# A Strassen-type first stage whose input sums get a buffer for the third sum and start at the first plain product, and whose weight differences are handed out in steps

## The chip, the cores and the metric

One core of one Trainium2 chip runs the whole program. The metric is the device time of one execution in microseconds (us). Engines are named as in the profile: PE (TensorE, matrix products; PEld is its weight load), DVE (VectorE), ACT (ScalarE), POOL (GpSimd) and SP (SyncE, which here only issues transfers). The kernel before takes 853.27 us, the median of 3 runs (851.54 to 855.01).

## The reference

Inputs are float32 and the products are wanted to float32 accuracy. What matters here is the middle of three parts:

```python
attn = softmax(q @ k^T / 8 + bias)          # B=2, H=8, S=576, D=64
x = (attn @ v) as [N=1152 tokens, 512]
for e in range(4):                          # first stage, w1[e]: 512x1024, w2[e]: 1024x512
    h = max(x @ w1[e], 0)
    out += p[:, e:e+1] * (h @ w2[e])
h = out @ w_in                              # second stage, w_in: 512x2048, w_out: 2048x512
g = (a0 + a1*h + a2*h^2 + a3*h^3) / (1 + |b0||h| + |b1|h^2 + 1e-6)
return g @ w_out
```

`p` are the normalised shares of the four experts.

## The kernel before, in words

Accuracy comes from splitting: a float32 matrix is held as a high part in the PE's reduced float32 format and a low part (value minus high), and a product is three products, high*high, high*low and low*high. A split costs one ACT copy (high) and one subtraction on DVE or POOL (low).

The program has three phases. The bias and attention come first, ordered by a planner with costs and due times (`Flow`). At its end `x` lies in SBUF, transposed, as four blocks `x[b, c]`: b is the batch half (576 tokens) and c the half of the 512 input channels, each with a high and a low part of [128, 2, 576] (k = 0, 1 are the two 128-channel slices). Then comes `first_stage`, whose order is written out by hand, and then `second_stage`.

`first_stage` goes through 16 pairs p of hidden blocks: pair p is 256 of the 4096 hidden columns, two blocks f of 128. A pair's "up" part makes h for both f and both b; its "down" part `down(p, t)` (L853) is six 512-column products for token tile t = 0..8, after which DVE adds `prob * ps` to `acc` (L865 for p = 0, L867 after that). Pairs 0 and 1 are "plain": `plain(p, f, b)` (L896) is 24 products of 288 columns into PSUM bank x or y by turns. Pairs 2 to 15 use a Strassen-type scheme, `seven(p)` (L971): seven block products of 12 matmuls instead of eight, on blocks of x and on sums of blocks:

- s1 = x10 + x11, s2 = s1 - x00, s4 = x01 - s2 and s3 = x00 - x10 (each split into high and low);
- the order of the seven products by what they read is x00, x01, s2, s1, s3, s4, x11; they accumulate in the two banks x and y, so that a bank is begun again only after DVE and ACT have taken what was in it. `keep` (L964, ACT) copies a bank into the temporaries m1, u2 or m5, `finish` (L968, DVE) adds one of these to a bank, and `relu` (L891 ACT, and later L892 DVE through `late` and `flush`) writes h in two parts. The next pair's first product starts bank y anew, so it waits for L892 of the last product.

Between two of the seven products stands one `down` of the pair before; after the seventh stand two more (t = 7 and 8).

Three kinds of side work are put between these by hand, each on the in-order queues of DVE, ACT and POOL:

- `sum_steps` (L928) makes the sums in 36 steps, one instruction each: `whole` (L917, high plus low, DVE), `combine` (L920, DVE), `high` (L923, ACT) and `low` (L926, on DVE for k = 0, on POOL for k = 1). `tick(n)` (L1004) issues the next n steps. The third sum s3 is written over x[1, 0], so its steps stand last, after the last plain product has been issued.
- `conv_f64` (L305) turns the second stage's float64 weights into float32, five steps for a piece: ACT L313, DVE L315, L317, L319, L321, and then a store from SP. It uses `tick` too once the sums are done.
- `load_w` (L250) splits the weights of a later pair: ACT L273 and POOL L277 for the down weights, and `load_differences` (L281) for the up weights of pairs 2 and later, which the scheme needs as seven blocks, four of them differences: four POOL subtractions (L290), three ACT copies (L293, on 256, 512 and 1024 elements), three POOL subtractions for the low parts (L295, same sizes), and then `stage_w`, which has SP fetch a later chunk of weights into the staging buffer that came free. Within a pair `load_w` stands after the second product (down weights) and after the fourth (the next pair's up weights, all of it at once).

Of the kernel before, what the change touches and what calls it, by code (L numbers as in the profile page):

```python
# [18 lines left out]
B, H, S, D, HID = 2, 8, 576, 64, 32  # L19
# [4 lines left out]
NPAIR = E * FF // 256  # L24
P = 128
# [99 lines left out]
class Kernel:  # L125
# [124 lines left out]
    def load_w(self, n=1, defer=lambda fn: fn()):  # L250


        for _ in range(n):
            if self.w_next < len(self.w_plan):
                i = self.w_next
                self.w_next += 1
                key, _, a, b = self.w_plan[i]
                stg = self.w_staged.pop(0)
                if key[0] == "u" and len(key) == 2 and key[1] > 1:
                    self.load_differences(key, stg)  # L260
                else:
                    self.load_parts(i, key, a, b, stg, defer)

    def load_parts(self, i, key, a, b, stg, defer):
        nc = self.nc
# [12 lines left out]
            self.stage_w()  # L278
        defer(low)

    def load_differences(self, key, stg):  # L281


        nc = self.nc
        wu = self.w_tiles[key] = self.up.tile([P, 2, 7, 2, P], F32R, tag="wu", bufs=2, name="wu")
        wt = self.up.tile([P, 4, 2, P], F32, tag="wt", bufs=1, name="wt")
        blocks = stg.rearrange("p (x k) (n f) -> p x n k f", x=2, n=2)
        (a, b), (c, d) = ([blocks[:, x, n] for n in range(2)] for x in range(2))
        for out, x, y in ((0, b, a), (2, d, b), (1, d, wt[:, 0]), (3, c, wt[:, 1])):
            nc.gpsimd.tensor_tensor(out=wt[:, out], in0=x, in1=y, op=ALU.subtract)  # L290
        parts = ((slice(0, 1), blocks[:, 0, 0:1]), (slice(1, 3), blocks[:, 1]), (slice(3, 7), wt))
        for sl, x in parts:
            nc.scalar.activation(out=wu[:, 0, sl], in_=x, func=AF.Copy)  # L293
        for sl, x in parts:
            nc.gpsimd.tensor_tensor(out=wu[:, 1, sl], in0=x, in1=wu[:, 0, sl].bitcast(F32), op=ALU.subtract)  # L295
        self.stage_w()

    def stage_f64(self):
# [570 lines left out]
    def first_stage(self):  # L869
# [3 lines left out]
        nc = self.nc  # L873
# [3 lines left out]
        def flush():  # L877
            while late:
                late.pop(0)()
# [16 lines left out]
        def plain(p, f, b):  # L896
            if b == 0:
                self.h_pair(p, f)
            ps = bank("xy"[plain_no[0] % 2])
            plain_no[0] += 1  # L900
            for half in range(2):
                for k in range(4):
                    self.up_part(ps[:, half, 0:288], p, f, b, half, k)
            flush()
            relu(p, f, b, ps[:, :, 0:288], True)

        sums = self.up.tile([P, 3, 2, 2, S], F32R, tag="s", bufs=1, name="sums")
        s1, s2, s4 = ((sums[:, i, 0], sums[:, i, 1]) for i in range(3))  # L910
        s3 = self.x[1, 0]

        def temp(tag):
            return self.up.tile([P, S], F32, tag=tag, bufs=1, name=tag)

        def whole(t, x, k):
            nc.vector.tensor_tensor(out=t, in0=x[0][:, k].bitcast(F32), in1=x[1][:, k].bitcast(F32), op=ALU.add)  # L917

        def combine(t, x, y, op):
            nc.vector.tensor_tensor(out=t, in0=x, in1=y, op=op)  # L920

        def high(t, s, k):
            nc.scalar.activation(out=s[0][:, k], in_=t, func=AF.Copy)  # L923

        def low(t, s, k):
            (nc.vector, nc.gpsimd)[k].tensor_tensor(out=s[1][:, k], in0=t, in1=s[0][:, k].bitcast(F32), op=ALU.subtract)  # L926

        def sum_steps():  # L928
            x = self.x
            for k in range(2):  # L930
                t, v, w = temp("m1"), temp("u2"), temp("m5")
                yield whole(t, x[1, 0], k)
                yield whole(v, x[1, 1], k)
                yield combine(t, t, v, ALU.add)
                yield high(t, s1, k)
                yield whole(v, x[0, 0], k)
                yield low(t, s1, k)
                yield combine(v, t, v, ALU.subtract)
                yield high(v, s2, k)
                yield whole(w, x[0, 1], k)  # L940
                yield low(v, s2, k)
                yield combine(w, w, v, ALU.subtract)
                yield high(w, s4, k)
                yield low(w, s4, k)
            for k in range(2):
                t, v = temp("m5"), temp("u3")
                yield whole(t, x[0, 0], k)
                yield whole(v, x[1, 0], k)
                yield combine(t, t, v, ALU.subtract)
                yield high(t, s3, k)  # L950
                yield low(t, s3, k)

        def product(ps, p, x, i, start, stop):
            wu = self.w_tiles["u", p]
            for k in range(2):
                for j, (w, v) in enumerate(((0, 0), (0, 1), (1, 0))):
                    for half in range(2):
                        nc.tensor.matmul(ps[:, half, 0:288], lhsT=wu[:, w, i, k], rhs=x[v][:, k, 288 * half:288 * half + 288],  # L958
                                         start=(start and k == j == 0), stop=(stop and k == 1 and j == 2), skip_group_check=True)
            flush()  # L960

        def keep(ps, tag):
            m = temp(tag)
            nc.scalar.activation(out=two(m), in_=ps[:, :, 0:288], func=AF.Copy)  # L964
            return m
# [5 lines left out]
        def seven(p):  # L971


            x = self.x
            self.h_pair(p, 0)
            self.h_pair(p, 1)
            y = bank("y")
            product(y, p, x[0, 0], 0, True, False)
            m1 = keep(y, "m1")
            yield  # L980
            z = bank("x")
            product(z, p, x[0, 1], 1, True, True)
# [12 lines left out]
            product(z, p, s4, 2, False, True)  # L995
            finish(p, 1, 0, z, u2)
            yield
            product(y, p, x[1, 1], 6, False, True)
            relu(p, 0, 1, y[:, :, 0:288], True)
            yield  # L1000

        side = sum_steps()

        def tick(n=1):  # L1004
            for _ in range(n):
                next(side, None)

        plain(0, 1, 0)
        self.load_w()
        plain(1, 0, 0)  # L1010
        plain(1, 1, 0)
        plain(0, 0, 1)
        tick(2)
        plain(0, 1, 1)
        tick(2)
        flush()
        self.load_w()
        for t in range(9):
            if t in (3, 6):
                plain(1, t // 3 - 1, 1)  # L1020
                tick(2)
            flush()
            self.down(0, t)
            tick(1 if t > 5 else 3)
            if t == 2:
                self.load_w()
        flush()
        self.stage_f64()
        self.stage_f64()
        for p in range(2, NPAIR):  # L1030
            for i, _ in enumerate(seven(p)):
                if p == 2 and i == 2:
                    assert next(side, 0) == 0
                    side = self.conv_f64()
                tick(3 if p == 2 and i < 2 else 1)
                flush()
                self.down(p - 1, i)
                tick(3 if p == 2 and i < 2 else i < 5)
                if i == 1 or i == 3 and p < NPAIR - 1:
                    self.load_w()  # L1040
            if p < NPAIR - 1:
                self.down(p - 1, 7)
                self.down(p - 1, 8)
# [193 lines left out]
```

## Time and profile before

| | us |
|---|---|
| median of 3 runs | 853.27 (851.54 to 855.01) |
| the profiled execution, its own time | 850.36 |
| its span in the trace | 848.5 |
| PE busy in the span | 803.2 (95%) |
| DVE busy | 696.9 (82%) |
| ACT busy | 500.0 (59%) |
| POOL busy | 469.4 (55%) |

The profiled execution took 1.9 us more than its span. Busy times are sums over instructions; the four engines work at the same time. The plain products of pairs 0 and 1 begin at 233.31 us in the span, pair 2 at 270.58 us, and the last of pair 15's seven products at 606.47 us. Idle time is given in the trace with the instruction that ended it.

### The profile page before, as it was taken

The page shows a single profiled execution, that of the slowest core. Times are in us where ns is not written, and L with a number is a line of the kernel's source. Part 1 is how long each engine was busy: PE and PEld are TensorE (multiplying, and loading weights), DVE is VectorE, ACT ScalarE, POOL GpSimd, SP SyncE. Part 2 cuts the span into 40 slices and gives each one's busy share as a digit, 9 for nine tenths or more (in the row PEclk, how much of TensorE's full clock was granted, in tenths as well). Part 3 has the DMA queues.
Part 4 walks back from the last instruction along what each step waited for, and adds up shares of the span by engine and source line. Part 5 has one row for each costly group of instructions (what it writes and reads, how often), then busy time and mean ns, then how long its engine had stood idle before and what let it go on. Part 6 is the DMA issues. An engine that isn't in the chain of part 4 may idle for free.

```text
span 848.5 us, 13528 instructions
## 1 busy us (share of the span) xinstructions
PE 803.2 (95%) x4980; PEld 691.7 (82%) x4980; DVE 696.9 (82%) x1162; ACT 500.0 (59%) x932; POOL 469.4 (55%) x398
## 2 busy tenths in 40 slices
PE   6989999998998899999999999999999899899997
PEld 2438888887897798888889889888888799789996
DVE  7978888888649888878988788889678878888885
ACT  6998898887523333333333333332368787878773
POOL 3287777777237544344555544344158977565552
PEclk9999999999999899999999999999999899999999
DMA  6777757461003143334343433334121211000011
GB/s 170 245 275 203 181 112 182 108 180 51 1 25 100 34 144 112 122 124 124 125 133 124 142 111 100 125 124 124 51 100 50 100 51 51 0 1 1 1 38 74
DMA packets 67522, 87.36 MB, mean 103 GB/s; under 512 B 33409, under 2 KB 41985, under 8 KB 67329
## 3 DMA queue, kind: packets, MB, share of 16 engines
q1 hardware_dynamic: 66880, 86.35, 33.7%
q8 instruction: 39, 0.64, 0.3%
q14 instruction: 27, 0.21, 0.1%
q10 hardware_dynamic: 576, 0.16, 0.1%
HBM read 60.12 MB, written 21.36 MB: 96 GB/s over the span
## 4 chain that ended last, share of the span: by engine, by line
PE 47%; DVE 20%; ACT 16%; issue 10%; POOL 6%; DMA 1%; SPq 0%; POOLq 0%; DVEq 0%; ACTq 0%
PE ps_o L861 11%; PE ps_y L958 6%; PE ps L660 5%; PE ps_o L1110 5%; PE ps_x L958 5%; PE ps_h L1102 5%; PE ps L550 3%; PE ps L610 3%; DVE pp L1091 2%; DVE rr L1090 2%; ACT rr L1087 2%; POOL qq L1085 2%; ACT hid L369 2%; DVE hs L892 2%; ACT bo L398 2%
## 5 line engine op out<-in xcount | busy, mean ns | idle before, releaser
L861 PE MATMUL ps_o<-we,hs 128*128 128x512 f32 x810 | 204.5, 394 | 0.0
L861 PEld LDWEIGHTS ps_o<-we,hs 128*128 128x128 f32 x810 | 146.9, 189 | 26.0
L277 POOL TENSOR_TENSOR we<-wstg,we 128x1024 fp32r<-128x1024 f32 x20 | 49.4, 2468 | 188.7 <-ACT we L273 188.7
L867 DVE SCALAR_TENSOR_TENSOR acc<-ps_o,prob,acc 128x512 f32<-128x512 f32 x135 | 98.2, 743 | 21.8 <-PE ps_o L861 21.6
L1085 POOL TENSOR_TENSOR qq<-qq,ha 128x384 f32<-128x384 f32 x48 | 58.4, 1216 | 66.2 <-ACT qq L1082 66.2
L1110 PE MATMUL ps_o<-wmh,hs 128*128 128x512 f32 x252 | 85.2, 396 | 9.3 <-POOL hs L1094 5.3
L958 PEld LDWEIGHTS ps_y<-x,wu 128*128 128x128 f32 x504 | 70.6, 188 | 9.3 <-DVE hs L892 6.7
L958 PE MATMUL ps_y<-x,wu 128*128 128x288 f32 x504 | 74.4, 296 | 2.8 <-DVE hs L892 2.5
L593 POOL TENSOR_SCALAR P<-P,ri 128x576 f32<-128x576 f32 x72 | 53.3, 752 | 39.4 <-DVE ri L582 26.9
L1102 PE MATMUL ps_h<-x,wmh 128*128 128x384 f32 x288 | 75.0, 341 | 0.0
L1110 PEld LDWEIGHTS ps_o<-wmh,hs 128*128 128x128 f32 x252 | 47.8, 190 | 21.7 <-POOL hs L1094 7.0
L564 DVE CUSTOM_DVE_ANT_0 P<-ps,bias 128x576 f32<-128x576 f32 x72 | 53.4, 749 | 10.8 <-PE ps L550 10.3
L572 ACT ACTIVATE P<-P,nm 128x576 f32<-128x576 f32 x72 | 55.6, 774 | 9.2 <-DVE nm L564 7.2
L1089 DVE SCALAR_TENSOR_TENSOR qq<-qq,rr 128x384 f32<-128x384 f32 x48 | 33.0, 688 | 30.1 <-ACT rr L1088 28.8
L380 PE MATMUL ps_ab<-hid,wm 128*32 128x288 f32 x576 | 47.7, 426 | 9.8 <-DVE hid L372 7.6
L1094 POOL TENSOR_TENSOR hs<-pp,hs 128x384 fp32r<-128x384 f32 x48 | 52.6, 1096 | 7.2 <-issue 6.2
L641 DVE TENSOR_TENSOR ptl<-ps,pth 128x512 fp32r<-128x512 f32 x72 | 51.1, 725 | 6.4 <-ACT pth L637 5.4
L1102 PEld LDWEIGHTS ps_h<-x,wmh 128*128 128x128 f32 x288 | 53.7, 192 | 2.0
L958 PE MATMUL ps_x<-sums,wu 128*128 128x288 f32 x336 | 50.4, 300 | 3.9 <-DVE m L968 3.9
L958 PEld LDWEIGHTS ps_x<-sums,wu 128*128 128x128 f32 x336 | 48.7, 193 | 6.4 <-DVE m L968 4.3
L550 PE MATMUL ps<-kh,qs 128*128 128x288 f32 x168 | 51.6, 327 | 1.2 <-DVE nm L564 0.8
L372 DVE TENSOR_SCALAR hid<-ltab,shift 128x576 f32<-128x576 f32 x108 | 50.2, 541 | 0.0
(145 smaller groups left out, 2054.9 us busy)
## 6 DMA issues: line engine op xcount, KB each, us to landing
wstg<-moe_w SPq DMA_DIRECT2D x32, 512.0 KB, 3.6
bias_d<-bo SPq DMA_DIRECT2D x9, 1152.0 KB, 5.1
bias<-bias_d SPq DMA_DIRECT2D x16, 576.0 KB, 5.0
w<-moe_w_in SPq DMA_DIRECT2D x16, 512.0 KB, 4.0
w<-moe_w_out SPq DMA_DIRECT2D x16, 512.0 KB, 3.7
kl<-kh SPq DMA_DIRECT2D x16, 288.0 KB, 4.8
w_u<-wmag SPq DMA_DIRECT2D x16, 256.0 KB, 2.3
w_d<-wmag SPq DMA_DIRECT2D x16, 256.0 KB, 2.4
```

What stands on the lines that cost most here:

```text
L550: nc.tensor.matmul(ps[:, half, dst:dst + w], lhsT=lhs, rhs=k[:, src:src + w], start=(i == 0), stop=(i == len(m) - 1))
L564: nc.vector.tensor_tensor_reduce(out=Pt[u][:, S * h:S * h + S].rearrange("p (a b) -> p a b", a=2), in0=ps[:, :, 0:288], in1=self.bias_t[n ...
L572: nc.scalar.activation(out=pt, in_=pt, func=AF.Exp, scale=-1.0, bias=stat.pop(g), accum_out=sums[n, c][:, h:h + 1])
L593: nc.gpsimd.tensor_scalar(out=pt[:, sl], in0=pt[:, sl], scalar1=ri, scalar2=1.0, op0=ALU.mult, op1=ALU.mult)
L641: nc.vector.tensor_tensor(out=dl, in0=ps, in1=dh.bitcast(F32), op=ALU.subtract)
L861: nc.tensor.matmul(ps, lhsT=a, rhs=w[:, f, :], start=(f == i == 0), stop=(f == 1 and i == 2))
L867: nc.vector.scalar_tensor_tensor(out=acc[:, t], in0=ps, scalar=pr, in1=acc[:, t], op0=ALU.mult, op1=ALU.add)
L958: nc.tensor.matmul(ps[:, half, 0:288], lhsT=wu[:, w, i, k], rhs=x[v][:, k, 288 * half:288 * half + 288], start=(start and k == j == 0), st ...
L1085: nc.gpsimd.tensor_tensor(out=qq, in0=qq, in1=ha, op=ALU.mult)
L1094: nc.gpsimd.tensor_tensor(out=lo, in0=pp, in1=hi.bitcast(F32), op=ALU.subtract)
L1102: nc.tensor.matmul(ps, lhsT=w[:, k, fo:fo + P], rhs=v[:, k, :], start=(k == i == 0), stop=(k == 3 and i == 2))
L1110: nc.tensor.matmul(ps, lhsT=a[:, P * tt:P * tt + P], rhs=w[:, f % 2, :], start=(f == i == 0), stop=(f == 3 and i == 2))
```

## The change

The buffer `sums` gets a fourth slot, and s3 is written there instead of over x[1, 0]. The steps of the sums are put in another order, 32 in place of 36: the whole blocks x10 and x00 are reused, so four `whole` steps fall away; the low parts of s1 and s2 are made on DVE for both k, those of s3 and s4 on POOL. The steps begin behind the first plain product, three behind each of the first five plain products, two behind each of the others, then two for each of the first six down tiles and one for each of the last three; all are out before pair 2. `conv_f64` therefore has the ticks of pair 2 from its first product on, and from here on its ticks stand on both sides of the down tile for products 0 to 5 and nowhere at product 6 (before: ahead of the down tile for all seven, behind it for the first five).

`load_differences` becomes a generator. In a pair it is opened after the second product, and its pieces are issued after the third (the four POOL subtractions), the fourth (first ACT copy), the fifth (second ACT copy) and the sixth (third ACT copy, all three POOL low parts, and the fetch). For pair 2's own weights it is still run through at once, in `load_w` at t == 2.

```diff
-                    self.load_differences(key, stg)
+                    self.w_next -= 1
+                    for _ in self.load_differences():
+                        pass
...
         for out, x, y in ((0, b, a), (2, d, b), (1, d, wt[:, 0]), (3, c, wt[:, 1])):
             nc.gpsimd.tensor_tensor(out=wt[:, out], in0=x, in1=y, op=ALU.subtract)
-        parts = ((slice(0, 1), blocks[:, 0, 0:1]), (slice(1, 3), blocks[:, 1]), (slice(3, 7), wt))
-        for sl, x in parts:
-            nc.scalar.activation(out=wu[:, 0, sl], in_=x, func=AF.Copy)
-        for sl, x in parts:
-            nc.gpsimd.tensor_tensor(out=wu[:, 1, sl], in0=x, in1=wu[:, 0, sl].bitcast(F32), op=ALU.subtract)
+        yield
+        high(0)
+        yield
+        high(1)
+        yield
+        high(2)
+        for i in range(3):
+            low(i)
         self.stage_w()
...
-        sums = self.up.tile([P, 3, 2, 2, S], F32R, tag="s", bufs=1, name="sums")
-        s1, s2, s4 = ((sums[:, i, 0], sums[:, i, 1]) for i in range(3))
-        s3 = self.x[1, 0]
+        sums = self.up.tile([P, 4, 2, 2, S], F32R, tag="s", bufs=1, name="sums")
+        s1, s2, s3, s4 = ((sums[:, i, 0], sums[:, i, 1]) for i in range(4))
...
             for k in range(2):
-                t, v, w = temp("m1"), temp("u2"), temp("m5")
+                t, v, w, u = (temp(tag) for tag in ("m1", "u2", "m5", "u3"))
                 yield whole(t, x[1, 0], k)
                 yield whole(v, x[1, 1], k)
-                yield combine(t, t, v, ALU.add)
...
+                yield combine(v, t, v, ALU.add)
+                yield high(v, s1, k)
+                yield whole(w, x[0, 0], k)
+                yield combine(t, w, t, ALU.subtract)
+                yield high(t, s3, k)
+                yield low(v, s1, k, nc.vector)
+                yield combine(v, v, w, ALU.subtract)
+                yield high(v, s2, k)
+                yield low(t, s3, k, nc.gpsimd)
+                yield whole(u, x[0, 1], k)
+                yield low(v, s2, k, nc.vector)
+                yield combine(u, u, v, ALU.subtract)
+                yield high(u, s4, k)
+                yield low(u, s4, k, nc.gpsimd)
...
         plain(0, 1, 0)
+        tick(3)
         self.load_w()
-        plain(1, 0, 0)
...
+        for p, f, b in ((1, 0, 0), (1, 1, 0), (0, 0, 1), (0, 1, 1)):
+            plain(p, f, b)
+            tick(3)
         flush()
...
-            tick(1 if t > 5 else 3)
+            tick(1 if t > 5 else 2)
...
+        side = self.conv_f64()
         for p in range(2, NPAIR):
+            weights = iter(())
             for i, _ in enumerate(seven(p)):
-                if p == 2 and i == 2:
-                    assert next(side, 0) == 0
-                    side = self.conv_f64()
-                tick(3 if p == 2 and i < 2 else 1)
+                tick(i < 6)
                 flush()
                 self.down(p - 1, i)
-                tick(3 if p == 2 and i < 2 else i < 5)
-                if i == 1 or i == 3 and p < NPAIR - 1:
+                tick(i < 6)
+                if i == 1:
                     self.load_w()
+                    if p < NPAIR - 1:
+                        weights = self.load_differences()
+                elif i > 1:
+                    next(weights, None)
```

## Rows read from the trace of the kernel before

**Rows 1.** PE's waits from 225 to 610: us in total, times, longest.

```profile
PE ps_x L958 <- DVE m L968: 3.9, 1, 3.9
PE ps_y L958 <- DVE hs L892: 2.5, 5, 0.6
PE ps_o L861 <- DVE acc L865: 2.1, 2, 1.3
```

**Rows 2.** Timeline of PE, pair 2 and start of pair 3: start, duration, line, shapes, [idle before].

```profile
270.58 1.75 PE L958 MATMUL ps_y<-x,wu 128*128 128x288 f32 x12
...
277.43 1.75 PE L958 MATMUL ps_y<-sums,wu 128*128 128x288 f32 x12
...
284.44 3.25 PE L958 MATMUL ps_x<-sums,wu 128*128 128x288 f32 x12 [3.88 <-DVE m L968]
...
290.03 1.75 PE L958 MATMUL ps_y<-x,wu 128*128 128x288 f32 x12
...
293.01 1.75 PE L958 MATMUL ps_x<-sums,wu 128*128 128x288 f32 x12
...
301.66 1.75 PE L958 MATMUL ps_y<-x,wu 128*128 128x288 f32 x12
```

**Rows 3.** Windows: busy us of PE, PEld, DVE, ACT, POOL; granted clock; DMA share, GB/s.

```profile
230.00:240.00 10.00, 10.00 (x64) 9.07 (x63) 1.74 (x3) 2.50 (x5) 2.89 (x3) 0.90 0.00 0
...
264.00:270.58 6.58, 4.53 (x19) 3.07 (x18) 6.55 (x8) 0.83 (x2) 4.37 (x3) 1.00 0.25 80
...
284.44:290.03 5.59, 5.59 (x19) 5.03 (x19) 4.79 (x5) 4.21 (x7) 5.33 (x4) 0.50 0.03 2
663.00:676.00 13.00, 9.21 (x32) 7.71 (x31) 11.36 (x13) 10.60 (x20) 13.00 (x9) 0.74 0.30 96
```

**Rows 4.** Timeline of DVE, sums and first pair.

```profile
244.50 0.75 DVE L917 TENSOR_TENSOR m<-x 128x576 f32<-128x576 f32 x1
...
252.22 2.95 DVE L926 TENSOR_TENSOR sums<-m,sums 128x576 fp32r<-128x576 f32 x1
...
283.63 0.75 DVE L968 TENSOR_TENSOR m<-ps_x,m 128x576 f32<-128x576 f32 x1
```

**Rows 5.** Timelines of PE, ACT and POOL in the plain part.

```profile
246.12 3.34 PE L851 MATMUL ps_x<-x,we 128*128 128x288 f32 x24
...
250.05 0.68 ACT L923 ACTIVATE sums<-m 128x576 fp32r<-128x576 f32 x1
...
261.69 1.04 ACT L293 ACTIVATE wu<-wt 128x1024 fp32r<-128x1024 f32 x1
262.64 0.63 ACT L891 ACTIVATE hs<-ps_y 128x576 fp32r<-128x576 f32 x1
...
251.75 2.80 POOL L277 TENSOR_TENSOR we<-wstg,we 128x1024 fp32r<-128x1024 f32 x1 [10.89 <-ACT we L273]
254.51 2.47 POOL L290 TENSOR_TENSOR wt<-wstg 128x256 f32<-128x256 f32 x2
...
268.37 1.41 POOL L926 TENSOR_TENSOR sums<-m,sums 128x576 fp32r<-128x576 f32 x1 [1.41 <-ACT sums L923]
```

**Rows 6.** Timeline of PE, last down tiles of pairs 2, 3 and 15.

```profile
297.56 4.26 PE L861 MATMUL ps_o<-we,hs 128*128 128x512 f32 x18
...
321.04 4.26 PE L861 MATMUL ps_o<-we,hs 128*128 128x512 f32 x18
...
608.05 4.26 PE L861 MATMUL ps_o<-we,hs 128*128 128x512 f32 x18
```

**Rows 7.** Timelines of POOL, DVE and PE at the end of pair 3.

```profile
318.07 2.91 POOL L295 TENSOR_TENSOR wu<-wt,wu 128x1024 fp32r<-128x1024 f32 x1
...
319.31 1.97 DVE L317 TENSOR_SCALAR wmag<-wmag 128x512 uint32<-128x512 uint32 x1
321.19 0.75 DVE L968 TENSOR_TENSOR u<-ps_x,u 128x576 f32<-128x576 f32 x1
...
324.63 0.75 DVE L892 SCALAR_TENSOR_TENSOR hs<-ps_y,hs 128x576 fp32r<-128x576 f32 x1
```

More of the change, by code (lines that the diff above doesn't have):

```diff
@@ L257, in load_w @@
                 key, _, a, b = self.w_plan[i]
-                stg = self.w_staged.pop(0)
                 if key[0] == "u" and len(key) == 2 and key[1] > 1:
-                    self.load_differences(key, stg)
+                    self.w_next -= 1
+                    for _ in self.load_differences():
+                        pass
                 else:
-                    self.load_parts(i, key, a, b, stg, defer)
+                    self.load_parts(i, key, a, b, self.w_staged.pop(0), defer)
     def load_parts(self, i, key, a, b, stg, defer):
@@ L279, in load_parts, with load_differences @@
         defer(low)
-    def load_differences(self, key, stg):
+    def load_differences(self):
         nc = self.nc
+        key = self.w_plan[self.w_next][0]
+        assert key[0] == "u"
+        self.w_next += 1
+        stg = self.w_staged.pop(0)
         wu = self.w_tiles[key] = self.up.tile([P, 2, 7, 2, P], F32R, tag="wu", bufs=2, name="wu")
@@ L288, in load_differences, with high, low @@
         (a, b), (c, d) = ([blocks[:, x, n] for n in range(2)] for x in range(2))
+        parts = ((slice(0, 1), blocks[:, 0, 0:1]), (slice(1, 3), blocks[:, 1]), (slice(3, 7), wt))
+        def high(i):
+            sl, x = parts[i]
+            nc.scalar.activation(out=wu[:, 0, sl], in_=x, func=AF.Copy)
+        def low(i):
+            sl, x = parts[i]
+            nc.gpsimd.tensor_tensor(out=wu[:, 1, sl], in0=x, in1=wu[:, 0, sl].bitcast(F32), op=ALU.subtract)
         for out, x, y in ((0, b, a), (2, d, b), (1, d, wt[:, 0]), (3, c, wt[:, 1])):
             nc.gpsimd.tensor_tensor(out=wt[:, out], in0=x, in1=y, op=ALU.subtract)
-        parts = ((slice(0, 1), blocks[:, 0, 0:1]), (slice(1, 3), blocks[:, 1]), (slice(3, 7), wt))
-        for sl, x in parts:
-            nc.scalar.activation(out=wu[:, 0, sl], in_=x, func=AF.Copy)
-        for sl, x in parts:
-            nc.gpsimd.tensor_tensor(out=wu[:, 1, sl], in0=x, in1=wu[:, 0, sl].bitcast(F32), op=ALU.subtract)
+        yield
[6 more added lines that the diff above has]
+            low(i)
         self.stage_w()
@@ L923, in high, with low @@
             nc.scalar.activation(out=s[0][:, k], in_=t, func=AF.Copy)
-        def low(t, s, k):
-            (nc.vector, nc.gpsimd)[k].tensor_tensor(out=s[1][:, k], in0=t, in1=s[0][:, k].bitcast(F32), op=ALU.subtract)
+        def low(t, s, k, eng):
+            eng.tensor_tensor(out=s[1][:, k], in0=t, in1=s[0][:, k].bitcast(F32), op=ALU.subtract)
         def sum_steps():
@@ L930, in sum_steps @@
             for k in range(2):
-                t, v, w = temp("m1"), temp("u2"), temp("m5")
+                t, v, w, u = (temp(tag) for tag in ("m1", "u2", "m5", "u3"))
                 yield whole(t, x[1, 0], k)
                 yield whole(v, x[1, 1], k)
-                yield combine(t, t, v, ALU.add)
[L935 to L938, printed above, removed]
-                yield high(v, s2, k)
[L940 to L951, printed above, removed]
+                yield combine(v, t, v, ALU.add)
[5 more added lines that the diff above has]
+                yield combine(v, v, w, ALU.subtract)
+                yield high(v, s2, k)
+                yield low(t, s3, k, nc.gpsimd)
[4 more added lines that the diff above has]
+                yield low(u, s4, k, nc.gpsimd)
         def product(ps, p, x, i, start, stop):
@@ L1008, in first_stage @@
         plain(0, 1, 0)
+        tick(3)
         self.load_w()
-        plain(1, 0, 0)
[L1011 to L1015, printed above, removed]
+        for p, f, b in ((1, 0, 0), (1, 1, 0), (0, 0, 1), (0, 1, 1)):
+            plain(p, f, b)
+            tick(3)
         flush()
@@ L1027, in first_stage @@
         flush()
+        assert next(side, 0) == 0
         self.stage_f64()
         self.stage_f64()
+        side = self.conv_f64()
         for p in range(2, NPAIR):
+            weights = iter(())
             for i, _ in enumerate(seven(p)):
-                if p == 2 and i == 2:
-                    assert next(side, 0) == 0
-                    side = self.conv_f64()
-                tick(3 if p == 2 and i < 2 else 1)
+                tick(i < 6)
                 flush()
                 self.down(p - 1, i)
-                tick(3 if p == 2 and i < 2 else i < 5)
-                if i == 1 or i == 3 and p < NPAIR - 1:
+                tick(i < 6)
+                if i == 1:
                     self.load_w()
+                    if p < NPAIR - 1:
+                        weights = self.load_differences()
+                elif i > 1:
+                    next(weights, None)
             if p < NPAIR - 1:
```

## The prediction

> **What bounds the kernel now.** I read the page's busy shares first: PE is busy for 95% of the span, so only what PE loses can be won. Of the 40 slices the change touches those from 233 to 610 us. Next come PE's own waits there: only three lines, 8.5 us together [rows 1]. The longest, 3.9 us, is a Strassen product on `sums` that waits for the DVE addition L968.
>
> The timeline of PE puts a price on it [rows 2]. One product with its down tile takes 293.01 - 290.03 = 2.98 us where nothing disturbs. The s2 product starts at 277.43, so PE is free at 280.41; the s1 product starts at 284.44: a gap of 4.0 us. The window behind it shows a granted clock of 0.50, that is 1.2 in place of 2.4 GHz [rows 3]: this step takes 290.03 - 284.44 = 5.59, 2.61 us too long. Pair 2 lasts 301.66 - 270.58 = 31.08 us; from the last down tiles of pair 2 to those of pair 3 it is 321.04 - 297.56 = 23.48 us, a pair with almost no stall [rows 6]. Pair 2 therefore loses 7.6 us: 4.0, 2.6 and 1.0 in small gaps.
>
> Why is the addition late? It needs only the second product, long done. On DVE the steps of s3 stand ahead of it, and each chain of whole, combine, high, low there waits for ACT and comes back; it starts at 283.63 [rows 4]. Pair 2 waits for side work queued ahead on DVE, not for its inputs.
>
> Two smaller losses: ahead of pair 2 the down tiles wait 2.1 us for L865 [rows 1]. And the 13 steps from pair 2's end to pair 15's take 608.05 - 297.56 = 310.49, against 13 x 23.48 = 305.2: 5.3 us, 0.4 a pair [rows 6]. These are the waits for L892, the low part of the last product in bank y.
>
> **The sums.** Now the first step starts at 244.50 [rows 4], though DVE was busy for only 1.74 us between 230 and 240 [rows 3]. After the change the first steps come about 234.5. The plain products stand 3.2 us apart: the first of five begins at 233.31, the last at 246.12 [rows 5]. In the time of one, DVE has at most three steps of 0.66 (instructions of 0.75 [rows 4] overlap a little) and one L892: 2.7 us, which fits. One of the steps meets the POOL low part of the down weights at 238.5 and may take up to 2.95, as L926 did at 252.22 [rows 4]; there is slack for it. So after the fifth product all of k = 0 is done but s4's low part, and PE never waited.
>
> For k = 1 I lay the queues out with today's durations. POOL: down weights from 251.75 [rows 5], then s4's low (1.41 [rows 5], some 1.9 with a DVE step in between), then the four differences from 256.4 in place of 254.51, until 261.0. ACT's third copy waits for these, 261.1 to 262.1 (today 261.69 [rows 5]), then the relu of the plain product, which stands behind it today too (262.64 [rows 5]), to 262.7; L892 to 263.4; the accumulation of tile 3 to 264.1. Then s1's low and a combine, each waiting out a POOL instruction (266.0, 267.9), then tile 4's accumulation, 268.6. Down tile 7 is on time; tile 8, ready at 266.5, starts at 268.7. One gap of 2.2 us replaces today's two with 2.1; as nothing else is late, pair 2 starts at 270.1 in place of 270.58: 0.4 us won (between none and 2.1).
>
> Last sums: s3's low 267.4, s2's 270.6, s4's high 272.0 and its POOL low 273.6. They are due at 276, 279, 282 and 285 (s2, s1, s3, s4; 2.98 us a step from 270.1). The smallest margin, s2's, is 5 us, so even several colliding steps don't bring a sum late. Pair 2 then runs like any pair: 31.1 becomes 23.5 to 23.9. I take 7.5 us; bounds: 7.6, and 6 if conv_f64, which now also ticks in the first two products, costs a gap of its own (eight ticks become twelve, about 0.7 us of DVE work each).
>
> Four `whole` steps less, 2.7 us of DVE, were in the stalled stretch and are in that figure already. The fourth slot costs 9.2 KB a partition and no instruction; freshly laid out memory could make the first temporaries wait for attention's last readers, which end by 236: under 2 us of idle DVE, nothing on PE.
>
> **The weights in steps.** Where do the 0.4 us a pair go today? At the end of pair 3 POOL's long low part runs 318.07 to 320.98; the short conv step L317 waits it out (1.97 us); so the addition of u2 comes at 321.19 [rows 7], though its product ended at 318.1 (a step of 2.98 us ahead of the last tiles' 321.04 [rows 6]); two relus, a low part, an accumulation and a conv step follow, and L892 from 324.63 to 325.38 [rows 7], while PE was ready at 325.1 (321.04 and three tiles of 1.4). The wait is one DVE instruction with only SBUF operands queued behind one POOL instruction.
>
> After the change the long POOL part can't start before ACT's third copy, which stands behind the relu of u2. Laid out: product ends 318.1, addition 318.4 to 319.1, relu to 319.7, copy (1.04 [rows 5]) to 320.7, POOL low 320.8 to 323.2 (2.91 [rows 7] less some 0.5 that it waited itself). On DVE: low part of u2 to 320.5, accumulation to 321.1, the second conv tick of this product, which now meets the POOL low and ends at 323.8, and L892 at 324.5: before 325.1, no wait. The fetch moves with POOL, to the pair's end; its 512 KB chunk lands some 4 us later (the page's list of transfers) and is wanted behind the third product of the next pair, 9 us on. The first two copies on ACT, 0.4 and 0.6 us, stand in gaps of ACT.
>
> The margin is 0.6 us, and conv's five steps meet 12 ticks a pair, so the pattern repeats every five pairs. Where the addition itself is late by a collision with the smaller POOL low parts the wait stays: laid out over five pairs, 0.8, 0, 0, 0.3 and 0 us. In 13 pairs that is 3 us against 5.3, less 0.07 a pair that my laid-out pair is longer than the 23.48: 1.5 us won. Bounds: 5.3 won, if no wait is left; a loss with the second rival.
>
> Here a rule speaks against the change. L317's 1.97 us [rows 7] shows the exclusion of DVE and POOL. The Trainium skill (SBUF — State Buffer, "Who interferes with whom") says that a DVE instruction in a two-port mode, or with two SBUF inputs against a POOL instruction that reads SBUF, and the POOL instruction lock each other out for the whole of one; the trace agrees. By it nothing is won from spreading as such: the second rival.
>
> **Sum.** 7.5 + 0.4 + 1.5 = 9.4 us. The profiled execution's own 850.36 us, 1.9 us around its span, becomes 841. The median of the runs is 2.9 us above it, so 853.27 - 9.4 = 843.9.
>
> **Rivals.**
> First, the small waits all vanish: 7.6 + 2.1 + 5.3 = 15, 838.3 us. For it: they all come from collisions whose places move. Against: 2.2 us ahead of pair 2 is a chain through POOL, ACT and DVE that the change doesn't shorten. Chance 0.11.
>
> Second, slower: the pair's end becomes the bound. Place: the conv tick between the last two low parts, behind the long POOL part. If the addition of u2 came as late as today, 321.2, POOL would run 323.6 to 326.1, the tick to 326.7, L892 to 327.4 and PE would wait 2.3 us, 2 more than now; in all 13 pairs +26, less 8 won ahead of them: 871; from 0.6 us more a pair on the gain is gone. For it: four of five phases put a DVE step there. Against: the addition is late today because of the very POOL part that moves behind it. Chance 0.06.
>
> Third, the gap of 2.2 us ahead of pair 2 lowers the clock, 2.6 us as in pair 2, and pairs end no better than now: 9.4 - 2.6 - 1.5 = 5.3, 848 us. For it: from 663 to 676, with gaps of about 2 us close together, the granted clock is 0.74; against: 1.00 from 264 to 270.58 with 2.1 us in two gaps [rows 3]. The Trainium skill (TensorE: Matmul & The Clock Gate, "HAM oscillation — how this bites in real kernels") says that idle gaps bring the lower clock back; the 0.50 of [rows 3] agrees, and for one such gap no run here shows it. Chance 0.15.
>
> Fourth, the change doesn't do what it says: pair 2 still waits, for its weights' low parts on POOL or an addition queued behind another late step. By the layout POOL has them at 265.4 and the third product wants them at 276, so I give it 0.07; about 852 us.
>
> **How the numbers follow.** The forecast, 843.9 us, has 0.61, with 841 to 847 as its own range. The range 839 to 849.5 takes in the third rival and the upper edge of the first; it leaves out the rest of that, the second and the fourth, some 0.18. A measurement tells 0.5%, 4.3 us: faster is the forecast, the first and most of the third, 0.85; same is the fourth and the rest of the third, 0.09; slower 0.06.
>
> **What would show it.** Right: PE's wait for L968 is gone, the granted clock is 1.00 from 240 to 300, the span from pair 2's first product to pair 3's is under 24.5 us, sum steps start before 240, and the 13 steps from pair 2's end to pair 15's take 306 to 310 us. Wrong: a wait of over 1 us at the s2, s1, s3 or s4 product, a low clock ahead of pair 2, or L892 waits above 0.4 us a pair; the first would bring down the main term.

## The result

The changed kernel takes 840.92 us (median of 4 runs, 840.66 to 841.87), the kernel before 852.40 in the runs beside it: a ratio of 0.9871, 95% interval 0.9831 to 0.9910, so 7.7 to 14.4 us less. Timed again later it took 843.86 against 850.07 us (0.9916, 0.9888 to 0.9945), so 4.7 to 9.5 us less. The forecast, 9.4 us less, lies inside the first span and at the edge of the second. The profiled execution takes 841.87 us, its span is 839.8: 8.7 us less than the span before.

Executions of one kernel differ by several us here, and the mean granted clock goes with it (in the later set one execution took 839.58 us at 0.991, another 847.18 at 0.982); the profiles have their stretches of low PE clock at different places. The stages of a trace repeat better, to about 1 us or less, so I compare stages. A is from the first plain product to pair 2's first product, B from there to pair 2's last down tiles, C the 13 steps to pair 15's, D the rest to the end of the span; the forecast's row is the kernel before less the prediction's 0.4, 7.5 and 1.5.

| us | A | B | C | D |
|---|---|---|---|---|
| before | 37.27 | 26.98 | 310.49 | 240.45 |
| after | 37.27 | 20.44 | 308.48 | 240.38 |
| forecast for after | 36.9 | 19.5 | 309.0 | 240.45 |

Each entry is a difference of starts in the timeline of PE, as 270.50 - 233.23 = 37.27. So 6.5 us came from pair 2, 2.0 from the pairs' ends, and nothing from the stage ahead of pair 2.

PE's waits after the change, from 225 to 610 (the lines that answer to [rows 1]):

```profile
PE ps_o L879 <- DVE acc L883: 1.8, 1, 1.8
PE ps_y L971 <- DVE hs L910: 1.8, 5, 0.4
```

The 3.9 us line, the product that waited for the addition (L968 before, L981 now), is gone. The waits at the down tiles (now L883) and at bank y (now L910) are smaller. The timeline of PE around pair 2 answers to [rows 2] and [rows 6]:

```profile
233.23 3.44 PE L869 MATMUL ps_x<-x,we 128*128 128x288 f32 x24
...
268.49 0.50 PE L879 MATMUL ps_o<-wdh,hs 128*128 128x512 f32 x1 [1.82 <-DVE acc L883]
...
270.50 2.79 PE L971 MATMUL ps_y<-x,wu 128*128 128x288 f32 x12
273.13 1.55 PE L879 MATMUL ps_o<-we,hs 128*128 128x512 f32 x6
...
277.49 1.75 PE L971 MATMUL ps_y<-sums,wu 128*128 128x288 f32 x12
...
280.45 1.75 PE L971 MATMUL ps_x<-sums,wu 128*128 128x288 f32 x12
...
290.94 4.26 PE L879 MATMUL ps_o<-we,hs 128*128 128x512 f32 x18
295.04 1.75 PE L971 MATMUL ps_y<-x,wu 128*128 128x288 f32 x12
...
599.42 6.99 PE L879 MATMUL ps_o<-we,hs 128*128 128x512 f32 x30
```

The s2 and the s1 product stand 280.45 - 277.49 = 2.96 us apart; before it was 7.0. But one gap is left at the last down tile, and pair 2's first product takes 2.63 us to its down tile (273.13) in place of 1.58. The windows say why (columns as in [rows 3]):

```profile
230.00:240.00 10.00, 10.00 (x64) 9.10 (x64) 6.55 (x8) 2.57 (x5) 3.91 (x3) 0.91 0.00 0
...
269.10:272.60 3.50, 3.50 (x14) 3.16 (x13) 3.50 (x6) 0.69 (x1) 0.71 (x1) 0.54 0.35 74
```

DVE now works for 6.55 of the 10 us from 230 on, where it worked for 1.74. And behind the gap the granted clock is 0.54: almost all of this stretch is at 1.2 GHz.

The queues ahead of pair 2, DVE, then ACT, then POOL, answer to [rows 4] and [rows 5]:

```profile
234.33 0.76 DVE L934 TENSOR_TENSOR m<-x 128x576 f32<-128x576 f32 x1
...
238.86 2.83 DVE L937 TENSOR_TENSOR m<-m,m 128x576 f32<-128x576 f32 x1
...
262.60 0.76 DVE L910 SCALAR_TENSOR_TENSOR hs<-ps_y,hs 128x576 fp32r<-128x576 f32 x1 [3.07 <-ACT hs L909]
263.28 0.74 DVE L883 TENSOR_SCALAR acc<-ps_o,prob 128x512 f32<-128x512 f32 x1
263.94 1.94 DVE L943 TENSOR_TENSOR sums<-u,sums 128x576 fp32r<-128x576 f32 x1
265.91 1.86 DVE L937 TENSOR_TENSOR u<-u,m 128x576 f32<-128x576 f32 x1
267.69 1.40 DVE L883 TENSOR_SCALAR acc<-ps_o,prob 128x512 f32<-128x512 f32 x2
...
260.97 1.06 ACT L298 ACTIVATE wu<-wt 128x1024 fp32r<-128x1024 f32 x1 [2.43 <-POOL wt L305]
261.94 0.63 ACT L909 ACTIVATE hs<-ps_y 128x576 fp32r<-128x576 f32 x1
...
256.34 2.58 POOL L305 TENSOR_TENSOR wt<-wstg 128x256 f32<-128x256 f32 x2
258.88 2.06 POOL L305 TENSOR_TENSOR wt<-wstg,wt 128x256 f32<-128x256 f32 x2
...
271.89 1.43 POOL L943 TENSOR_TENSOR sums<-u,sums 128x576 fp32r<-128x576 f32 x1 [4.74 <-ACT sums L940]
```

The first sum step starts at 234.33. The last, s4's low part, is done at 273.3, and the s4 product starts at 286.39. The gap's chain can be read upward: POOL's differences until 260.9, ACT's third copy, the relu behind it, L910 (DVE idle for 3.07 us ahead of it), one accumulation, and two sum steps that each wait for a POOL instruction, then the accumulation that tile 8 waits for.

The end of pair 3, POOL, DVE and PE, answers to [rows 7]:

```profile
315.39 2.40 POOL L302 TENSOR_TENSOR wu<-wt,wu 128x1024 fp32r<-128x1024 f32 x1 [2.70 <-ACT wu L298]
...
311.61 1.37 DVE L333 TENSOR_SCALAR wmag<-wmag 128x512 f32<-128x512 f32 x1
312.90 0.74 DVE L981 TENSOR_TENSOR u<-ps_x,u 128x576 f32<-128x576 f32 x1
...
315.73 2.60 DVE L337 SCALAR_TENSOR_TENSOR wmag<-w,wmag 128x512 uint32<-128x512 uint32 x1
318.26 0.75 DVE L910 SCALAR_TENSOR_TENSOR hs<-ps_y,hs 128x576 fp32r<-128x576 f32 x1
318.92 2.05 DVE L885 SCALAR_TENSOR_TENSOR acc<-ps_o,prob,acc 128x512 f32<-128x512 f32 x3
...
319.06 1.87 PE L971 MATMUL ps_y<-x,wu 128*128 128x288 f32 x12 [0.37 <-DVE hs L910]
```

This is one of the five pair ends in 13 that still wait. POOL's long low part has moved behind the addition, and the conv step L337 now waits it out, 2.60 us, directly ahead of L910. The other eight come at 23.5 us a pair, as 314.42 to 290.94. A listed wait of 0.37 us makes its pair 0.65 us longer (24.13), so the 1.8 us listed stand for 3.2 us of C.

### The profile page after: what moved, and what is told of

Same layout as the page of the kernel before. It is cut to its first block, busy times and chain, and to the rows that moved or that the text cites. A ratio compares the mean times of both kernels' runs of the same rounds, so it can differ in the third digit from the quotient of the medians.

```text
span 839.8 us, 13520 instructions
## 1 busy us (share of the span) xinstructions
PE 801.3 (95%) x4980; PEld 692.4 (82%) x4980; DVE 689.3 (82%) x1158; ACT 499.6 (59%) x932; POOL 462.3 (55%) x398
## 4 chain that ended last, share of the span: by engine, by line
PE 45%; ACT 21%; DVE 21%; issue 6%; POOL 5%; DMA 1%; DVEq 0%; POOLq 0%; SPq 0%; ACTq 0%
PE ps_o L879 14%; PE ps_y L971 8%; PE ps_x L971 6%; PE ps L678 5%; ACT rr L1102 3%; POOL qq L1100 3%; PE ps L568 3%; ACT rr L1103 3%; DVE pp L1106 3%; DVE rr L1105 3%; PE ps L628 3%; DVE qq L1104 2%; ACT qq L1097 2%; ACT hid L387 2%; ACT hs L1108 2%
## 5 line engine op out<-in xcount | busy, mean ns | idle before, releaser
L885 DVE SCALAR_TENSOR_TENSOR acc<-ps_o,prob,acc 128x512 f32<-128x512 f32 x135 | 98.6, 743 | 28.8 <-PE ps_o L879 28.6
L909 ACT ACTIVATE hs<-m 128x576 fp32r<-128x576 f32 x28 | 19.2, 686 | 81.1 <-DVE m L981 81.1
L302 POOL TENSOR_TENSOR wu<-wt,wu 128x1024 fp32r<-128x1024 f32 x14 | 33.8, 2412 | 37.5 <-ACT wu L298 37.5
L971 PEld LDWEIGHTS ps_y<-x,wu 128*128 128x128 f32 x336 | 48.3, 193 | 5.8 <-DVE hs L910 3.9
L971 PE MATMUL ps_y<-x,wu 128*128 128x288 f32 x336 | 50.5, 300 | 1.8 <-DVE hs L910 1.8
```

The costliest lines, as they stand in the source:

```text
L885: nc.vector.scalar_tensor_tensor(out=acc[:, t], in0=ps, scalar=pr, in1=acc[:, t], op0=ALU.mult, op1=ALU.add)
```

## The experiments

The theory: PE waited for side work that was queued ahead of what it needed; pair 2's stall goes with the place of the sum steps, the pairs' waits with the order of a conv step and POOL's long low part. All stages in one table, in the order of the runs; the last column is the median and the ratio to the kernel before on the same chip, with its 95% interval.

| run | A | B | C | D | us, ratio |
|---|---|---|---|---|---|
| sums only | 36.74 | 19.39 | 309.45 | 243.22 | 844.57, 0.9930 (0.9897 to 0.9962) |
| weights only | 39.73 | 26.82 | 307.54 | 240.39 | 847.84, 0.9940 (0.9914 to 0.9966) |
| early, no buffer | 34.66 | 24.52 | 307.58 | 240.49 | 843.36, 0.9900 (0.9855 to 0.9944) |
| buffer, late start | 39.42 | 20.85 | 309.34 | 240.52 | 845.80, 0.9933 (0.9902 to 0.9963) |
| steps, old conv ticks | 36.50 | 19.38 | 308.48 | 243.34 | 842.74, 0.9903 (0.9865 to 0.9941) |
| pair 2's weights in steps | 36.52 | 20.18 | 308.71 | 240.47 | 839.63, 0.9881 (0.9843 to 0.9918) |
| and the tick moved | 34.64 | 20.18 | 305.54 | 240.38 | 838.67, 0.9853 (0.9820 to 0.9885) |
| low part on ACT | 35.99 | 19.40 | 305.81 | 240.41 | 838.01, one run |
| after, again | 38.28 | 19.40 | 308.00 | 240.42 | 843.86, 0.9916 (0.9888 to 0.9945) |
| tick moved, again | 34.63 | 19.47 | 305.62 | 240.36 | 836.16, 0.9838 (0.9818 to 0.9858) |

In three rows A holds a first plain product at low clock, some 1.8 us longer than the 3.44 it lists elsewhere: weights only (5.32), pair 2's weights in steps (5.32), after again (5.19).

**Sums only.**

```diff
...
-            weights = iter(())
...
-                tick(i < 6)
+                tick()
                 flush()
                 self.down(p - 1, i)
-                tick(i < 6)
+                tick(i < 5)
-                if i == 1:
-                    self.load_w()
-                    if p < NPAIR - 1:
-                        weights = self.load_differences()
-                elif i > 1:
-                    next(weights, None)
+                if i == 1 or i == 3 and p < NPAIR - 1:
+                    self.load_w()
```

> The changed kernel with only its sums part: the fourth slot, the new order and the early start stay; the next pair's weight differences are issued all at once behind the fourth product and the conv ticks stand as before the change. Theory: the two parts add up, and this one holds all that was won up to pair 3: pair 2 about 24.5 us as in the changed kernel, the 13 steps from pair 2's end to pair 15's back at about 310.5 us, so 2 us above the changed kernel in the profile, about 843 us. Rival (the conv steps, which now run from pair 2's first product, are part of what shortened pair 2): pair 2 over 26 us, 845 us or more.

(The part left out moves the `yield`s of `load_differences`; `load_w` runs it through at once, so its order stays.) Pair 2 lasts 294.58 - 270.84 = 23.74 us: the whole stall goes with the sums part alone. The rival's time isn't met, but this run leaves the conv steps where they begin, at pair 2's first product, and so doesn't test it by itself; the run without the buffer, below, has them there too and keeps a gap of 3.4 us. C is 309.45, 1.0 over the changed kernel and not the 2 that was expected. D is 2.8 us longer than in most runs; of its last 22 us the window shows a granted clock of 0.91 where the changed kernel's shows 1.00:

```profile
820.00:842.00 22.00, 17.04 (x69) 13.44 (x67) 11.21 (x19) 7.69 (x15) 5.87 (x6) 0.91 0.19 72
```

The clock is not all of it: half of the 2.8 us is lost before the low clock begins, 0.6 of that in a longer wait of PE there (2.2 us in place of 1.7). D is as long in one other run, the old conv ticks (243.34), which has the same sums and the same ticks; the kernel before, with these ticks and the old sums, has 240.45. Why these two runs lose it is open.

**Weights only.**

```diff
...
-                tick(3 if p == 2 and i < 2 else 1)
+                tick(3 if p == 2 and i < 2 else i < 6)
                 flush()
                 self.down(p - 1, i)
-                tick(3 if p == 2 and i < 2 else i < 5)
-                if i == 1 or i == 3 and p < NPAIR - 1:
+                tick(3 if p == 2 and i < 2 else i < 6)
+                if i == 1:
                     self.load_w()
+                    if p < NPAIR - 1:
+                        weights = self.load_differences()
+                elif i > 1:
+                    next(weights, None)
```

> The kernel before with only the weights part: differences handed out in steps and the conv ticks of the change; the sums as before. Theory: the stall of pair 2 with its low clock stays (pair 2 near 31 us) and the 13 steps take about 308.5 us, 2 us under the kernel before, in the profile about 848.5 us. Rival (pair 2 was long because a whole block of weight work was issued in it): pair 2 drops by 3 us or more.

(The part left out makes `load_differences` the generator of the change.)

```profile
PE ps_x L976 <- DVE m L986: 3.9, 1, 3.9
```

Pair 2 lasts 302.18 - 271.25 = 30.93 us and PE waits 3.9 us for the addition as before. The rival falls. C gains 3.0 us where 2 were expected. The parts add up only roughly: on the kernel before the weights part is worth 3.0 us in C, behind the sums part 1.0. The sums part also shifts where conv's five steps stand when pair 3 begins, and so the pairs at whose ends something collides; that this is the reason for the difference was not tested by itself.

**The early start without the buffer.**

```diff
-        s1, s2, s3, s4 = ((sums[:, i, 0], sums[:, i, 1]) for i in range(4))
+        s1, s2, s4 = ((sums[:, i, 0], sums[:, i, 1]) for i in range(3))
+        s3 = self.x[1, 0]
...
-            tick(1 if t > 5 else 2)
+            tick((2, 2, 2, 2, 1, 0, 2, 3, 3)[t])
```

> The changed kernel with the sums' 36 old steps and without the fourth slot: s3 is written over x10 again, and its ten steps stand behind the last plain product, all of them ahead of pair 2; all other steps start at the first plain product. Theory (what counts is where the steps stand on DVE, not the buffer): no wait for the addition of the second product over 1 us, pair 2 under 26.5 us, within 2 us of the changed kernel. Rival (the buffer is what frees them): a gap of 3 to 4 us in pair 2 with the low clock behind it stays, 847 us or more.

(The part left out puts the 36 old steps back, with their old shares of DVE and POOL.) Theory and rival are each half right. No product waits for the addition, and the time is near the changed kernel's (843.36 against 840.92 and 843.86), not the rival's 847. But pair 2 lasts 28.6 us, not under 26.5: the rival's gap stays, 3.4 us with the low clock behind it, now at the s2 product. PE, then ACT:

```profile
277.96 3.25 PE L976 MATMUL ps_y<-sums,wu 128*128 128x288 f32 x12 [3.36 <-ACT m L982]
...
276.69 0.68 ACT L941 ACTIVATE x<-m 128x576 fp32r<-128x576 f32 x1 [3.61 <-DVE m L938]
277.28 0.63 ACT L982 ACTIVATE m<-ps_y 128x576 f32<-128x576 f32 x1
```

PE needs ACT to copy out bank y. That copy stands on ACT behind s3's last high part, which waits for s3's chain on DVE. So it is the same kind of wait on another queue. Without the fourth slot s3's ten steps can't be issued before the last plain product, so they crowd directly ahead of pair 2 here and stood in its first products before the change. Against the changed kernel's profile this version loses 4.1 us in B (5.1 against the runs without low clock there) and wins 2.6 in A, 34.66: only one sum step (L938, 1.93 us) stands ahead of the accumulation that tile 8 waits for, where the changed kernel has two (1.94 and 1.86), and the gap at tile 8 is gone. In stages the missing buffer costs; the medians don't separate the two kernels.

**The buffer with the old start.**

```diff
...
         plain(0, 1, 0)
-        tick(3)
         self.load_w()
-        for p, f, b in ((1, 0, 0), (1, 1, 0), (0, 0, 1), (0, 1, 1)):
-            plain(p, f, b)
-            tick(3)
+        plain(1, 0, 0)
+        plain(1, 1, 0)
+        plain(0, 0, 1)
+        tick(2)
+        plain(0, 1, 1)
+        tick(2)
...
-            tick(1 if t > 5 else 2)
+            tick(1 if t > 5 else 3)
...
```

(The last three steps stand in pair 2's first product.)

> The changed kernel with the old start of the sums: the fourth slot and the 32 new steps stay, but the first steps come behind the fourth plain product, two, then two, then three a down tile, the last three in pair 2's first product. Theory (the early start is what pays): laid out in queue order, the gaps at the down tiles ahead of pair 2 grow to about 4 us and pair 2 keeps some 2 us of gaps, so about 6 us over the changed kernel without the clock, 846 to 849 us with it. Rival (the buffer and the four steps less are enough): within 2 us of the changed kernel.

845.8 us, 4.9 us over the changed kernel's first median and 1.9 over its later one, so the medians alone wouldn't bring the rival down. The stages do: A is 39.42, 2.2 to 2.9 us over the changed kernel's and the runs that share its A, and A to C together are 3.4 us over its profile. Most of B is still won, 20.85: the buffer and the order break up the chain. But the crowd on DVE stands ahead of pair 2 instead:

```profile
PE ps_o L879 <- DVE acc L883: 3.2, 2, 2.7
```

Together with the run before it: each half of the sums part takes away a different wait. The buffer, the new order and the four steps less go together in these runs; what each is worth was not tested.

**The old conv ticks.**

```diff
-                tick(i < 6)
+                tick()
                 flush()
                 self.down(p - 1, i)
-                tick(i < 6)
+                tick(i < 5)
```

> The changed kernel with only the conv ticks put back: one ahead of the down tile for all seven products, one behind it for the first five. The differences stay in steps. Theory: what shortened the pairs is that the addition of the sixth product no longer meets POOL's long low part, so the 13 steps stay within 1 us of the changed kernel's 308.5 us, about 841 us. Rival (it is the conv tick taken away from the seventh product): the 13 steps go back to 309.5 us or more.

C is 308.48, to the digit what the changed kernel shows. Which side of the seventh product this conv step stands on made no difference; the rival falls. This run and the first differ only in the steps of the weights, 308.48 against 309.45: that is 1.0 us for the steps. Whether the conv step stands ahead of L910 or behind it is another matter, see below.

**Pair 2's weights in steps.**

```diff
             if t == 2:
-                self.load_w()
+                weights = self.load_differences()
+            if 1 < t < 7:
+                next(weights, None)
```

> The changed kernel with pair 2's own weight differences handed out in steps too, over the down tiles 2 to 6, so that the relu of the plain product behind tile 2 stands on ACT ahead of the copies. Theory: the gap of 2.2 us at down tile 8 comes from this relu, which waits behind ACT's third copy and so behind POOL's differences; with it goes the low clock that follows it, so pair 2 starts at 267.9 in place of 270.50 and lasts under 24.2 us, 3 us less in the profile, about 838 us. Rival (DVE is simply full there): the gap stays over 1.5 us, 840.5 us or more.

The gap at the down tiles is gone from PE's waits, and the rival falls; pair 2 lasts 24.40 us, a little over the 24.2 expected. A is 36.52 with 1.9 us of low clock in its first product; in the next kernel, which is the same up to pair 2, it is 34.64: 1.9 to 2.6 us under the changed kernel and the runs that share its A (36.50 to 37.27). The relu now stands ahead of the copies on ACT, in this next kernel's trace at 258.15 in place of 261.94:

```profile
258.15 0.64 ACT L909 ACTIVATE hs<-ps_y 128x576 fp32r<-128x576 f32 x1
...
261.27 0.40 ACT L298 ACTIVATE wu<-wstg 128x256 fp32r<-128x256 f32 x1
```

So DVE was not full there; it waited on ACT, which waited on POOL. B is 0.8 us longer than in the run with the old ticks; 0.5 of it is a wait of the second product for L910 and bank x. The next run has the same 20.18 and the same wait, its later profile 19.47 and none. The trace shows a cost of the edit: POOL's long low part now runs just ahead of pair 2 (267.80, 2.91 us, in the next run), a sum step waits it out (L937, 2.95 us) and L910 stands behind that step (271.26). In the later profile this chain is there too and ends 0.1 us before PE wants the bank.

**The moved tick.** As above, and the conv step between the last two low parts moves behind L910:

```diff
                 self.down(p - 1, i)
-                tick(i < 6)
+                tick(i != 5)
```

> As the run with pair 2's weights in steps, and the second conv tick of the sixth product is moved behind the down tile of the seventh, so that it stands behind L910 of bank y and no longer between the last two low parts. Theory: the waits that are left at the pairs' ends are this conv step waiting out POOL's long low part; the 13 steps fall from 308.5 to 305.5 us, about 835 us in all. Rival (the waits come from collisions earlier in the pair, or the moved step delays the next pair's start): the 13 steps stay over 307.5 us.

C is 305.54 us, against 13 x 23.48 = 305.2 with no wait at all; expected were 305.5 (the median, 838.67, is above the 835 expected). PE's waits for bank y are gone from the list. DVE, then POOL, at the end of the pair that is shown above:

```profile
312.93 0.75 DVE L885 SCALAR_TENSOR_TENSOR acc<-ps_o,prob,acc 128x512 f32<-128x512 f32 x1
313.74 0.76 DVE L910 SCALAR_TENSOR_TENSOR hs<-ps_y,hs 128x576 fp32r<-128x576 f32 x1
314.41 0.74 DVE L885 SCALAR_TENSOR_TENSOR acc<-ps_o,prob,acc 128x512 f32<-128x512 f32 x1
315.07 1.13 DVE L337 SCALAR_TENSOR_TENSOR wmag<-w,wmag 128x512 uint32<-128x512 uint32 x1
...
313.25 2.40 POOL L302 TENSOR_TENSOR wu<-wt,wu 128x1024 fp32r<-128x1024 f32 x1 [2.69 <-ACT wu L298]
```

L910 runs at its usual length while POOL works; it reads PSUM and one SBUF operand. Only the conv step behind it waits, and nobody waits for that.

**The long low part on ACT.**

```diff
-        for i in range(3):
+        for i in range(2):
             low(i)
+        nc.scalar.activation(out=wu[:, 1, 3:7], in_=wt, func=AF.Copy)
```

> The changed kernel with POOL's longest instruction of a pair, the low part of the four differences, replaced by a copy of the same size on ACT, so these low parts hold the differences themselves and the products are other numbers. Theory (DVE steps wait because POOL holds the memory port): with POOL idle at the pair's end no conv step there takes over 1 us, and the 13 steps fall to 306 us or less, though ACT has 1 us more a pair in front of the last relu. Rival (the last relu on ACT sets the pair's end): the 13 steps get longer than 308.5 us.

This kernel leaves out the subtraction of POOL's long part, so it shows only where time goes. C falls to 305.81 us with 1 us more a pair on ACT, and no wait for bank y is in PE's list; the conv step that took 2.60 us takes 0.68 there. The rival falls. Two different edits, one that takes POOL's instruction away and one that takes the conv step out of its way, both end the wait. That settles the cause of what is left in C.

**Again, side by side.**

> The changed kernel as it is, timed on one chip beside the version with both further steps. Theory: its stages repeat to 0.3 us, about 37 us from the first plain product to pair 2, 19.4 to 20.5 us to pair 2's last tiles and 308.5 us for the 13 steps; about 841 us and 10 us under the kernel before. Rival (part of the gain shown was one favourable set of runs): 845 us or more.

> The version with pair 2's weights in steps and the moved conv tick, timed on the same chip as the changed kernel. Theory: 2 us less ahead of pair 2 and 3 us less in the 13 steps, so about 5 us under the changed kernel's median. Rival (the time is given back in the second stage, whose low clock comes at another place): within 2 us of the changed kernel.

On one chip: 843.86 us for the changed kernel (between the 841 expected and the rival's 845), 836.16 for the version with both further steps, 7.7 us apart where 5 were expected; in the stages it is 1.9 us in A (with 1.75 of low clock in the changed kernel's first product taken off) and 2.4 in C. The rest is low clock ahead of pair 2, which this profile of the changed kernel has more of, 0.52 from 230 to 240 against 1.00 in the other version's:

```profile
230.00:240.00 10.00, 10.00 (x38) 8.68 (x37) 4.21 (x6) 0.86 (x2) 2.28 (x2) 0.52 0.00 0
```

The changed kernel's stages repeat less well than the 0.3 us expected: C to 0.5, and A and B to 1.0 each, as a low clock falls into A in one profile and behind the gap in the other. The version with both steps is the fastest here, 13.9 us under the kernel before.

## Why the prediction was right

The mechanism holds: 843.9 us forecast, 840.92 and 843.86 measured. That the total fits so well is in part luck: against the forecast the profile lost 0.4 us in A and 1.0 in B and won 0.5 in C. Nor does a stage show the 2.9 us by which the forecast's median stands above the profiled execution: the changed kernel's first median is 0.95 under its own, and the kernel before had medians from 850.07 to 853.27.

- Pair 2's stall, 7.5 us. Where no low clock follows the gap ahead of it, B is 19.38 to 19.40 (four runs with the same sums part), 7.6 us under the kernel before. In the profile of the changed kernel 1.05 us of that goes to the low clock, so it shows 6.5. The layout by queue order put the last sum at 273.6; it is there at 273.3. PE's list had one line more in this stage than the three that were read, 0.6 us for L892 at bank x; it is the 0.65 us ahead of pair 2's second product, and the 1.0 us of small gaps holds it.
- Ahead of pair 2, 0.4 us. The layout gave one gap, at tile 8, with a start at 268.7; it starts at 268.49. The profile shows A unchanged because of the clock behind the gap; the runs with the same A and none of this (36.50, 36.74) show 0.5 to 0.8 won.
- The low clock of the third rival came, in the profile shown, behind one gap of about 2 us. It did not come in three other profiles with the same gap (sums only, old conv ticks, after again). That a single gap may or may not bring it is more than the prediction knew. It cost about 1 us of pair 2 there and some 0.5 ahead of it, not 2.6, and the second half of that rival, pairs no better than before, did not come. Two signs of being right failed in this profile by it: the granted clock is not 1.00 throughout from 240 to 300, and pair 2 lasts 295.04 - 270.50 = 24.54 us, just over 24.5 (23.50 in the second profile).
- The pairs' ends, 1.5 us: 2.0 in the profile, 2.5 in the second one. Five waits in 13 pairs were laid out and there are five (four are listed in the second profile). The reason given for the pairs that still wait was the smaller POOL low parts delaying the addition. That is one half: L333 takes 1.37 us at 311.61 ahead of the addition, and then L337 another 2.60 at the long part. Moving the last alone ends the wait. The first counts too: at 362.25 another conv step, L335, takes 2.34 us at the long part, behind an addition that is on time, and PE does not wait.
- The Trainium skill (SBUF — State Buffer, "Who interferes with whom") says that a DVE instruction with two SBUF inputs and a POOL instruction that reads SBUF shut each other out, and that one with at most one SBUF input, outside the two-port modes, does not contend. The trace agrees: L337, two SBUF inputs, takes 2.60 us in one order and 0.68 at the same place with the POOL part gone; L910, one PSUM and one SBUF input, 0.76 beside POOL's 2.40. So spreading the work does not take collisions away; what counts is whether one stands ahead of what PE waits for.
- The weakest step was the split of the change into parts that add up. The weights part gave 1.0 or 3.0 us in C depending on what stood ahead of it.

## What to carry to other kernels

When a product waits for an instruction whose inputs were ready long ago, read the in-order queue of its engine, and then the queues of the engines that this queue waits for: side work put there by hand is a due time for everything behind it. Start such work where the engine is idle, give it a buffer if its output place forces it late, and hand out long pieces one at a time behind the instruction that the matrix engine waits for, not in front of it. Where DVE instructions with only SBUF operands share time with long POOL instructions, look at their order next to the critical one first: moving one conv step won as much here as taking the POOL instruction away (C 305.54 and 305.81 us, from about 308.5).

## What the runs showed of the hardware

- In the cases read here a DVE instruction with only SBUF operands that met a POOL instruction waited until that one ended: L337 2.60 us against 0.68, L937 2.83 from 0.5 us after the start of a POOL instruction of 2.69. POOL's long low part takes 2.40 us where nothing stood in its way and 2.91 [rows 7] where a DVE instruction had waited in front of it.
- PE's low clock moves the total by more than some edits. In three of twelve profiles the first plain product lists 5.2 or 5.3 us in place of 3.44 though nothing near it was changed. Between two profiles of the changed kernel the stages differ by 1.0 us (A and B), 0.5 (C) and 0.04 (D), its medians by 3.
